# Scaling a position bias as it leaves PSUM, and moving relus and key copies between engines

## The chip, the cores and the metric

The kernel runs on one core of one Trainium2 chip. The metric is the device time of one execution in microseconds; of several runs the median is taken.

## The reference

Three parts follow one another, all in float32, for B=4 batches, H=8 heads, S=576 positions, D=64.

```
rel  = pos[:, None] - pos[None, :]
x    = log1p(|rel|) / log1p(max(pos[:, None], 1))          # psi_rel / l(i)
bias = relu(x * w1 + b1) @ w2                              # (S, S, H), 32 hidden units
s    = q @ k.T / sqrt(64) + bias[h]
attn = softmax(s);  o = attn @ v
x    = o as (2304, 512);  h = x @ w_in;  x = max(0.01 h, h) @ w_out
out  = top-1 mixture of 8 experts, gate * (relu(x @ w1[e]) @ w2[e])
```

The bias doesn't depend on the batch. Because l(i) is positive, relu(w1 psi/l + b1) = (1/l) relu(w1 psi + b1 l), so that the factor 1/l(i) of a query row can be applied anywhere behind the relu.

## The kernel before

One stream of instructions for five engines is written by a Python program; a planner orders them and places the waits. The kernel's first phase, in which everything that the diff touches lies, does attention and the first large product.

*The bias.* It is made once, in 36 blocks of 16 query rows (`bias_units`, block `m`), and written to a table in HBM. A block's 16 rows are four groups of four: partition p stands for hidden unit p mod 32 of row group p div 32. For each group `q`, `bias_relu` makes a tile `mk` of max(lw + v, 0) with 304 to 576 columns, either on VectorE (L224) or on ScalarE (L222), as the table `RELU[m % 4][q]` says. TensorE then multiplies it by `cf`, the output weights already multiplied by 1/l(i) (L270), four groups side by side, into PSUM. `cf` is made on POOL for two blocks at once (L254) from `e.coef` and `e.br`, which holds 1/l(i) per row; it has two buffers. PSUM is copied to a tile `bt`: blocks below 12 or from 32 on as one piece of 591 columns on ScalarE, the others in two halves, the first on VectorE in even blocks, all else on ScalarE. [...] There are 11 buffers of `mk` and 5 of `bt`.

*Keys and queries.* Heads go in pairs. Products are done with each operand split in a high part (rounded to a faster format) and a low part (the rest). `kv_hi` rounds the keys of a pair, the even head on partitions 0 to 63 and the odd one on 64 to 127, into a tile `kt`; `k_lo` subtracts on VectorE (L82) and puts the low parts on the other 64 partitions; a last copy (L337) doubles the odd head's last 64 keys in front of it, because the odd head's columns are read in the order last 64, first 512. The engine of `kv_hi` is given per batch by `K_HI`: POOL for batch 0 (L74), ScalarE for the others (L70).

*Around it.* Sixteen blocks of bias are issued before the first attention step, with the keys and queries of the first two pairs; the other blocks fill the gaps of the first eight steps and are drained there. A step takes 128 query rows of a pair: load the bias rows, scores (L413), add and minimum (L418, VectorE), exp (L426, ScalarE), normalisation (L444 on POOL for batch 0, L440 and L442 on ScalarE and VectorE otherwise), transposes (L464, L486), values (L500). Meanwhile `w_in` and `w_out` arrive as 64-bit floats and are converted on VectorE (tiles `w_t`, L99, L103, L107) and split into `wi`. The up-projection (L525, `psh`) fills TensorE's gaps from the end of the first four pairs on. Later phases are the down-projection, the routing and the experts.

Of the kernel before, what the change touches and what calls it, by code (L numbers as in the profile page):

```python
# [7 lines left out]
F32 = mybir.dt.float32  # L8
# [5 lines left out]
AF = mybir.ActivationFunctionType  # L14
ALU = mybir.AluOpType
# [4 lines left out]
B, H, S, D = 4, 8, 576, 64  # L20
NP = H // 2
# [17 lines left out]
BC = S + 15  # L39
# [3 lines left out]


WIN_HI, WIN_LO = "DDAA", "DDDD"
K_HI, K_LO = "PAAA", "DDDD"
Q_HI, Q_LO = "AAAA", "DDDD"
PROB_T = ("ADDD", "AAAA")
X_HI = "DDDD"
NORM = ("PDDD", "PAAA")  # L50

RELU = ("DDAD", "DADD", "DAAD", "ADDA")

WIDE, RELU_BUFS, BIAS_BUFS, COEF_M = 12, 11, 5, 2

PROBS = 4

# [11 lines left out]
def copy_act(nc, out, in_):  # L69
    nc.scalar.activation(out=out, in_=in_, func=AF.Copy)  # L70
# [66 lines left out]
def host_constants():  # L137

    import numpy as np

    pos = np.arange(S).astype(np.float32)
    lg = np.log1p(pos)
    l = np.log1p(np.maximum(pos, np.float32(1.0)))
    p = np.arange(128)
    i1 = 4 * np.arange(144)[None, :] + (p // 32)[:, None]
    return {
        "c_lw": np.ascontiguousarray(np.broadcast_to(lg, (128, S))),
        "c_r": np.ascontiguousarray(np.concatenate([l[i1], np.float32(1.0) / l[i1]], axis=1)),
        "c_rt": np.ascontiguousarray(np.concatenate([
            np.broadcast_to(np.arange(128), (128, 128)),  # L150
            np.broadcast_to(np.arange(NSP), (128, NSP)),
            128 * np.arange(NTILE)[None, :] + p[:, None] + 1,
            np.broadcast_to(E - np.arange(E), (128, E)),
        ], axis=1).astype(np.float32)),
        "c_slot": (2.0 ** np.arange(NREST)).astype(np.float32)[None, :],
        "c_u": np.ascontiguousarray(np.concatenate([
            p[:, None] < p[None, :], np.ones((128, 128), bool)], axis=1).astype(np.float16)),
    }


def lay_out(q, k, v, w1, b1, w2):

    import numpy as np

    qt = q.reshape(B, NP, 2, S, D).transpose(0, 1, 4, 2, 3)
    kt = k.reshape(B, NP, 2, S, D).transpose(0, 1, 2, 4, 3).reshape(B, NP, 128, S)
    vp = v.reshape(B, NP, 2, S, D).transpose(0, 1, 3, 2, 4)
    main = vp[:, :, :512].reshape(B, NP, 4, 128, 2, D).transpose(0, 1, 3, 2, 4, 5)

    tail = np.zeros((B, NP, 128, 1, 2, D), v.dtype)  # L170
    for h in range(2):
        tail[:, :, 64 * h:64 * h + 64, 0, h] = vp[:, :, 512:, h]
    wb = np.concatenate([w1.reshape(HID, 1), b1.reshape(HID, 1), w2], axis=1)
    return {
        "in_q": np.ascontiguousarray(np.concatenate([qt, qt], axis=2)),
        "in_k": np.ascontiguousarray(kt),
        "in_v": np.ascontiguousarray(np.concatenate([main, tail], axis=3)),
        "in_wb": np.ascontiguousarray(np.concatenate([wb] * 4, axis=0)),
    }


def bias_setup(nc, e):

    sp = e.bout
    rr = sp.tile([128, 288], F32, name="rr")
    wb = sp.tile([128, 2 + H], F32, name="wb")
    e.lw = sp.tile([128, S], F32, name="lw")
    nc.sync.dma_start(out=wb, in_=e.wb)  # L190
    nc.scalar.dma_start(out=rr, in_=e.c_r)
    nc.sync.dma_start(out=e.lw, in_=e.c_lw)
    w1r, b1r, w2r = wb[:, 0:1], wb[:, 1:2], wb[:, 2:2 + H]
    sg = sp.tile([128, 4], F32, name="sg")
    sign, aw, ba, aw8 = (sg[:, k:k + 1] for k in range(4))
    nc.vector.tensor_scalar(out=sign, in0=w1r, scalar1=0.0, scalar2=2.0, op0=ALU.is_ge, op1=ALU.mult)
    nc.vector.tensor_scalar_add(sign, sign, -1.0)
    nc.vector.tensor_scalar(out=aw, in0=w1r, scalar1=sign, scalar2=1.0e-20, op0=ALU.mult, op1=ALU.max)
    nc.vector.tensor_scalar_mul(aw8, aw, 8.0)
    nc.vector.reciprocal(ba, aw)  # L200
    nc.vector.tensor_scalar_mul(ba, ba, b1r)
    e.bv = sp.tile([128, 144], F32, name="v")
    nc.vector.tensor_scalar_mul(e.bv, rr[:, 0:144], ba)
    e.br = rr[:, 144:288]
    nc.vector.tensor_scalar_mul(e.lw, e.lw, sign)

    e.coef = sp.tile([128, 4, H], F32, name="coef")
    nc.gpsimd.memset(e.coef, 0.0)
    for g in range(4):
        ps = slice(32 * g, 32 * g + 32)  # L210
        nc.vector.tensor_scalar_mul(e.coef[ps, g], w2r[ps], aw8[ps])


def bias_relu(nc, e, m, qs):

    out = []
    n = max(16 * m + 16, S - 16 * m)
    for q in qs:
        mk = e.bout.tile([128, S], F32, tag="mk", name="mk", bufs=RELU_BUFS)
        o, x, k = mk[:, :n], e.lw[:, :n], slice(4 * m + q, 4 * m + q + 1)  # L220
        if RELU[m % 4][q] == "A":
            nc.scalar.activation(out=o, in_=x, func=AF.Relu, bias=e.bv[:, k])  # L222
        else:
            nc.vector.tensor_scalar(out=o, in0=x, scalar1=e.bv[:, k], scalar2=0.0, op0=ALU.add, op1=ALU.max)  # L224
        out.append(mk)
    return out
# [16 lines left out]
def bias_units(nc, e, wide):  # L243

    nm = S // 16
    nxt = bias_relu(nc, e, 0, range(4))
    for m in range(nm):  # L250
        mk, nxt = nxt, []
        if m % COEF_M == 0:
            cf = e.bout.tile([128, 4 * COEF_M, 4 * H], F32, tag="cf", name="cf", bufs=2)
            nc.gpsimd.tensor_tensor(  # L254
                out=cf, in0=e.coef.rearrange("p g h -> p (g h)").unsqueeze(1).to_broadcast([128, 4 * COEF_M, 4 * H]),
                in1=e.br[:, 4 * m:4 * m + 4 * COEF_M].unsqueeze(2).to_broadcast([128, 4 * COEF_M, 4 * H]), op=ALU.mult,
            )
        bt = e.bout.tile([128, BC], F32, tag="bt", name="bt", bufs=BIAS_BUFS)
        both = m < wide or m >= 32
        o = 0 if m < 4 else 1024 - BC if m >= 32 else 496 - 16 * m  # L260
        pieces = bias_pieces(m, o)
        if both:
            ps2 = e.psS.tile([128, 2, 512], F32, tag="s", name="psb2").rearrange("p a j -> p (a j)")
        half = (len(pieces) + 1) // 2
        for hf in range(2):
            for a, b, d, falls in pieces[half * hf:half * hf + half]:
                ps = ps2[:, o + a:] if both else e.psM.tile([128, 512], F32, tag="m", name="psb")
                for q in range(4):
                    x = mk[q][:, d - (b - a) + 1:d + 1][:, ::-1] if falls else mk[q][:, d:d + b - a]
                    nc.tensor.matmul(  # L270
                        ps[32 * q:32 * q + 32, :b - a], lhsT=cf[:, 4 * (m % COEF_M) + q], rhs=x,
                        start=True, stop=True, tile_position=(0, 32 * q),
                    )
                if not both:
                    (copy_act if hf or m % 2 else copy_dve)(nc, bt[:, a:b], ps[:, :b - a])
            if m + 1 < nm:
                nxt += bias_relu(nc, e, m + 1, (2 * hf, 2 * hf + 1))
            if hf == 1:
                if both:
                    copy_act(nc, bt, ps2[:, o:o + BC])  # L280

                r0 = 16 * (m % 8) * BP
                dst = e.bias_d[m // 8][:, r0:r0 + 16 * (BP + 1)].rearrange("h (r c) -> r h c", c=BP + 1)
                nc.sync.dma_start(out=dst[:, :, :BC], in_=bt)
            yield 800


class Attention:
# [19 lines left out]

    def kv_load(self, b, p):
        nc, e = self.nc, self.e  # L310
        kr = e.raw.tile([128, S], F32, tag="kraw", name="kraw")
        nc.sync.dma_start(out=kr, in_=e.k[b, p])
        self.raw[b, p] = kr

# [6 lines left out]
    def kv_hi(self, b, p):  # L321
        nc, e = self.nc, self.e
        kr = self.raw[b, p]
        kt = e.kvp.tile([128, 1216], F32R, tag=f"kt{p}", name="kt", bufs=1)
        hi = COPY[K_HI[b]]
        hi(nc, kt[0:64, 0:576], kr[0:64])
        hi(nc, kt[64:128, 640:1216], kr[64:128])
        self.kv[b, p] = kt

    def k_lo(self, b, p):  # L330
        nc = self.nc
        kr = self.raw.pop((b, p))
        kt = self.kv[b, p]
        lo = LO[K_LO[b]]
        lo(nc, kt[64:128, 0:576], kr[0:64], kt[0:64, 0:576])
        lo(nc, kt[0:64, 640:1216], kr[64:128], kt[64:128, 640:1216])
        nc.vector.tensor_copy(kt[:, 576:640], kt[:, 1152:1216].bitcast(F32))  # L337


    def q_load(self, g):  # L340
# [222 lines left out]
def phase1(ctx, tc, e):  # L563
# [56 lines left out]

    bias_setup(nc, e)
    bu = bias_units(nc, e, WIDE)
    for k in range(32):
        if k == 20:
# [832 lines left out]
```

## Time and profile before

| what | us |
|---|---|
| median of 3 runs | 1030.96 (1027.31 to 1032.47) |
| the profiled execution | 1027.66 |
| its span | 1025.9 |
| TensorE matmul busy | 985.7 (96%) |
| VectorE busy | 682.8 (67%) |
| ScalarE busy | 547.8 (53%) |
| POOL busy | 103.0 (10%) |

PE is TensorE's matmuls and PEld its weight loads, DVE is VectorE, ACT ScalarE, POOL GpSimd and SP SyncE. The span is the part of the time in which instructions run. Busy shares are averages over stages with different limits: what an engine is worth in a stage is read from that stage. The durations of one line are given as minimum, median and maximum or as a mean; neighbours on an engine overlap a little, so that a sum of durations is somewhat more than the busy time.

### The profile page before, as it was taken

The page shows a single profiled execution, that of the slowest core. Times are in us where ns is not written, and L with a number is a line of the kernel's source. Part 1 is how long each engine was busy: PE and PEld are TensorE (multiplying, and loading weights), DVE is VectorE, ACT ScalarE, POOL GpSimd, SP SyncE. Part 2 cuts the span into 40 slices and gives each one's busy share as a digit, 9 for nine tenths or more (in the row PEclk, how much of TensorE's full clock was granted, in tenths as well). Part 3 has the DMA queues.
Part 4 walks back from the last instruction along what each step waited for, and adds up shares of the span by engine and source line. Part 5 has one row for each costly group of instructions (what it writes and reads, how often), then busy time and mean ns, then how long its engine had stood idle before and what let it go on. Part 6 is the DMA issues. An engine that isn't in the chain of part 4 may idle for free.

```text
span 1025.9 us, 19107 instructions
## 1 busy us (share of the span) xinstructions
PE 985.7 (96%) x6294; PEld 809.2 (79%) x6294; DVE 682.8 (67%) x1719; ACT 547.8 (53%) x1102; POOL 103.0 (10%) x112
## 2 busy tenths in 40 slices
PE   5899999999999999999999999999999999999995
PEld 2355788988889898998888888888877888888884
DVE  8888999889865687767675766579892255313312
ACT  5778787556665666556453333344552455324422
POOL 2332431000000000000000000001002111211210
PEclk9999999999999999999999999999998999999998
DMA  7868899989754566546195533338305256313410
GB/s 247 256 202 247 251 297 310 319 284 288 223 172 142 177 205 196 154 129 183 49 294 171 166 111 117 120 103 280 101 11 216 66 203 254 120 49 106 143 42 23
DMA packets 137602, 180.17 MB, mean 176 GB/s; under 512 B 19841, under 2 KB 89857, under 8 KB 137362
## 3 DMA queue, kind: packets, MB, share of 16 engines
q1 hardware_dynamic: 115554, 149.31, 46.9%
q10 hardware_dynamic: 18576, 19.03, 5.3%
q0 software_dynamic: 3360, 10.49, 3.0%
q8 instruction: 52, 0.85, 0.3%
q14 instruction: 60, 0.49, 0.2%
HBM read 196.18 MB, written 43.94 MB: 234 GB/s over the span
## 4 chain that ended last, share of the span: by engine, by line
PE 81%; DVE 7%; DMA 6%; issue 3%; ACT 1%; POOL 1%; SPq 0%; DVEq 0%; ACTq 0%; POOLq 0%
PE psx L784 19%; PE psh L525 15%; PE pu L1272 10%; PE pd L1303 9%; PE pss L413 7%; PE psv L500 7%; PE pst L464 5%; PE psb L270 3%; DMA wo_raw<-in_w_out_dram 3%; DVE mk L224 2%; PE pt L1283 1%; DMA w_t<-wo 1%; PE pt L1255 1%; DMA qraw<-in_q_dram 1%; PE psx L486 1%
## 5 line engine op out<-in xcount | busy, mean ns | idle before, releaser
L525 PE MATMUL psh<-x,wi 128*128 128x256 f32 (+1 forms) x1536 | 226.4, 297 | 1.4 <-DVE hst L532 1.3
L525 PEld LDWEIGHTS psh<-x,wi 128*128 128x128 f32 x1536 | 211.0, 189 | 3.6 <-DVE hst L532 2.9
L426 ACT ACTIVATE prob<-prob,stat 128x576 f32<-128x576 f32 x144 | 111.3, 773 | 66.2 <-DVE stat L418 58.7
L418 DVE CUSTOM_DVE_ANT_0 prob<-pss,prob 128x576 f32<-128x576 f32 x144 | 108.0, 752 | 20.5 <-PE pss L413 16.5
L784 PE MATMUL psx<-woh,gh 128*128 128x512 f32 x288 | 113.1, 393 | 0.3 <-ACT gh L70 0.3
L784 PE MATMUL psx<-wol,gh 128*128 128x512 f32 x288 | 112.7, 391 | 0.0
L784 PE MATMUL psx<-woh,gl 128*128 128x512 f32 x288 | 112.2, 390 | 0.0
L70 ACT ACTIVATE gh<-g 128x512 fp32r<-128x512 f32 x72 | 45.3, 631 | 115.2 <-PE psx L784 99.9
L464 PE MATMUL pst<-ident,prob 128*128 128x128 f32 x576 | 89.4, 278 | 4.4 <-DVE pth L78 2.1
L464 PEld LDWEIGHTS pst<-ident,prob 128*128 128x128 f32 x576 | 65.9, 140 | 23.0 <-issue 13.9
L1241 POOL DMA_INDIRECT xg<-x,gidx x22 | 25.3, 1152 | 577.6 <-DMA ws<-in_mw_dram 549.1
L413 PE MATMUL pss<-kt,qhi 128*128 128x288 f32 x256 | 81.3, 332 | 0.0
L270 PE MATMUL psb<-mk,cf 128*32 128x79 f32 (+49 forms) x640 | 60.8, 420 | 13.9 <-POOL cf L254 6.8
L413 PE MATMUL pss<-kt,qlo 128*128 128x288 f32 x256 | 72.3, 297 | 0.0
L500 PE MATMUL psv<-pth,vs 128*64 128x256 f32 (+1 forms) x512 | 72.1, 413 | 0.0
L1303 PE MATMUL pd<-w2h,hth 128*128 128x512 f32 x160 | 67.8, 424 | 3.9 <-ACTq L1228 3.9
L801 DVE SCALAR_TENSOR_TENSOR junk<-x1s,en 128x512 bf16<-128x512 f32 x96 | 66.1, 689 | 3.1 <-DMA en<-en_d 2.1
L82 DVE TENSOR_TENSOR htl<-pt,hth 128x512 fp32r<-128x512 f32 x40 | 27.1, 689 | 57.8 <-ACT hth L70 57.8
L70 ACT ACTIVATE pth<-pst 128x512 f32<-128x512 f32 (+1 forms) x100 | 54.4, 548 | 20.6 <-PE pst L464 12.8
L1272 PE MATMUL pu<-w1h,xh 128*128 128x512 f32 x160 | 65.1, 407 | 0.3 <-ACT xh L70 0.3
L1303 PE MATMUL pd<-w2h,htl 128*128 128x512 f32 x160 | 64.7, 404 | 0.0
L1303 PE MATMUL pd<-w2l,hth 128*128 128x512 f32 x160 | 64.3, 402 | 0.0
(224 smaller groups left out, 1869.3 us busy)
## 6 DMA issues: line engine op xcount, KB each, us to landing
ws<-in_mw_dram SPq DMA_DIRECT2D x164, 512.0 KB
prob<-bias SPq DMA_DIRECT2D x64, 288.0 KB
g<-h SPq DMA_DIRECT2D x72, 256.0 KB
prob<-bias SPq DMA_DIRECT2D x64, 256.0 KB
bias<-bt SPq DMA_DIRECT2D x36, 295.5 KB
h<-hst ACTq DMA_DIRECT2D x64, 160.0 KB
w_raw<-in_w_in_dram SPq DMA_DIRECT2D x16, 512.0 KB
h<-hst ACTq DMA_DIRECT2D x64, 128.0 KB
```

Of the source, the lines that this page charges most:

```text
L70: nc.scalar.activation(out=out, in_=in_, func=AF.Copy)
L270: nc.tensor.matmul(ps[32 * q:32 * q + 32, :b - a], lhsT=cf[:, 4 * (m % COEF_M) + q], rhs=x, start=True, stop=True, tile_position=(0, 32 * q),)
L413: nc.tensor.matmul(ps[:, jh, :288], lhsT=lhsT, rhs=kt[:, c0 + 288 * jh:][:, :288], start=(k == 0), stop=(k == len(ops) - 1),)
L418: nc.vector.tensor_tensor_reduce(out=prv, in0=ps[:, :, :288], in1=prv, scale=-0.125, scalar=3.0e38, op0=ALU.add, op1=ALU.min, accum_out=st ...
L426: nc.scalar.activation(out=pr[:, h], in_=pr[:, h], func=AF.Exp, bias=stat[:, 0, h:h + 1], scale=-1.0, accum_out=stat[:, 1, h:h + 1],)
L464: nc.tensor.transpose(ps[:, 128 * c:128 * c + 128], pr[:, h, 64 * h + 128 * c:][:, :128], e.ident)
L500: nc.tensor.matmul(ps[64 * h:64 * h + 64, :n], lhsT=vs[:, c, h], rhs=ph[:, h, c, :n] if c < 4 else pt[:, :n], start=(c == 0), stop=(c == 4 ...
L525: nc.tensor.matmul(ps[:, :n], lhsT=w[:, kc], rhs=x[:, kc, :n], start=(k == 0), stop=(k == 3 * KD - 1),)
L784: nc.tensor.matmul(ps, lhsT=a[:, c % 4], rhs=w[:, c], start=(k == 0), stop=(k == 3 * KF - 1))
L801: nc.vector.scalar_tensor_tensor(out=junk, in0=x1, scalar=1.0, in1=e.en[:, k], op0=ALU.mult, op1=ALU.mult, accum_out=e.dots[:, t, k:k + 1],)
L1272: nc.tensor.matmul(ps, lhsT=a[:, k], rhs=w[:, k, c], start=(i == 0), stop=(i == 3 * KD - 1))
L1303: nc.tensor.matmul(ps, lhsT=a[:, k], rhs=w[:, k], start=(k == 0 and j == 0), stop=(k == 7 and j == 2))
```

## The change

1. `cf` and its product on POOL (18 instructions) go. TensorE multiplies by the unscaled weights `e.coef`, the same for all blocks. The factor 1/l(i) is applied where PSUM is copied to `bt`, as a scale per partition: ScalarE's copy gets a scale from a pointer, VectorE's copy becomes a multiplication by a pointer. The constant 1/l(i) is laid out for that, 36 columns in place of 144.
2. The odd head's keys come from the host with the last 64 repeated in front, so that a pair's tile has 640 columns in place of 576 (the even head's are padded with zeros); the copy of L337 goes, and the odd head's rounding and subtraction take 640 columns.
3. In `RELU` ScalarE keeps one of four relus in each block, where it had one, one, two and two: 36 of 144 in place of 54.
4. Batch 0's keys are rounded on VectorE in place of POOL.

```diff
-K_HI, K_LO = "PAAA", "DDDD"
+K_HI, K_LO = "DAAA", "DDDD"
-RELU = ("DDAD", "DADD", "DAAD", "ADDA")
-WIDE, RELU_BUFS, BIAS_BUFS, COEF_M = 12, 11, 5, 2
+RELU = ("DDAD", "DADD", "DDDA", "ADDD")
+WIDE, RELU_BUFS, BIAS_BUFS = 12, 11, 5
...
+    i2 = 16 * np.arange(S // 16)[None, :] + (p // H)[:, None]
-        "c_r": np.ascontiguousarray(np.concatenate([l[i1], np.float32(1.0) / l[i1]], axis=1)),
+        "c_r": np.ascontiguousarray(np.concatenate([l[i1], np.float32(1.0) / l[i2]], axis=1)),
...
-    kt = k.reshape(B, NP, 2, S, D).transpose(0, 1, 2, 4, 3).reshape(B, NP, 128, S)
+    kp = k.reshape(B, NP, 2, S, D).transpose(0, 1, 2, 4, 3)
+    odd = np.concatenate([kp[:, :, 1, :, 512:], kp[:, :, 1]], axis=3)
+    even = np.concatenate([kp[:, :, 0], np.zeros_like(kp[:, :, 0, :, 512:])], axis=3)
+    kt = np.concatenate([even, odd], axis=2)
...
-        if m % COEF_M == 0:
-            cf = e.bout.tile([128, 4 * COEF_M, 4 * H], F32, tag="cf", name="cf", bufs=2)
-            nc.gpsimd.tensor_tensor(
-                out=cf, in0=e.coef.rearrange("p g h -> p (g h)").unsqueeze(1).to_broadcast([128, 4 * COEF_M, 4 * H]),
-                in1=e.br[:, 4 * m:4 * m + 4 * COEF_M].unsqueeze(2).to_broadcast([128, 4 * COEF_M, 4 * H]), op=ALU.mult,
-            )
+        scale = e.br[:, m:m + 1]
...
-                        ps[32 * q:32 * q + 32, :b - a], lhsT=cf[:, 4 * (m % COEF_M) + q], rhs=x,
+                        ps[32 * q:32 * q + 32, :b - a], lhsT=e.coef.rearrange("p g h -> p (g h)"), rhs=x,
...
-                    (copy_act if hf or m % 2 else copy_dve)(nc, bt[:, a:b], ps[:, :b - a])
+                    if hf or m % 2:
+                        nc.scalar.activation(out=bt[:, a:b], in_=ps[:, :b - a], func=AF.Copy, scale=scale)
+                    else:
+                        nc.vector.tensor_scalar_mul(bt[:, a:b], ps[:, :b - a], scale)
...
-                    copy_act(nc, bt, ps2[:, o:o + BC])
+                    nc.scalar.activation(out=bt, in_=ps2[:, o:o + BC], func=AF.Copy, scale=scale)
...
-        kr = e.raw.tile([128, S], F32, tag="kraw", name="kraw")
+        kr = e.raw.tile([128, S + 64], F32, tag="kraw", name="kraw")
...
-        hi(nc, kt[0:64, 0:576], kr[0:64])
-        hi(nc, kt[64:128, 640:1216], kr[64:128])
+        hi(nc, kt[0:64, 0:576], kr[0:64, :S])
+        hi(nc, kt[64:128, 576:1216], kr[64:128])
...
-        lo(nc, kt[64:128, 0:576], kr[0:64], kt[0:64, 0:576])
-        lo(nc, kt[0:64, 640:1216], kr[64:128], kt[64:128, 640:1216])
-        nc.vector.tensor_copy(kt[:, 576:640], kt[:, 1152:1216].bitcast(F32))
+        lo(nc, kt[64:128, 0:576], kr[0:64, :S], kt[0:64, 0:576])
+        lo(nc, kt[0:64, 576:1216], kr[64:128], kt[64:128, 576:1216])
```

## Rows read from the trace of the kernel before

**Rows 1.** The page's first part: busy us, share of the span, instructions.
```profile
PE 985.7 (96%) x6294; PEld 809.2 (79%) x6294; DVE 682.8 (67%) x1719; ACT 547.8 (53%) x1102; POOL 103.0 (10%) x112
```
**Rows 2.** Busy time by stage: PE, PEld, DVE, ACT, POOL, granted clock, DMA share, GB/s.
```profile
5.00:33.00 28.00, 19.96 (x214) 9.13 (x214) 27.56 (x54) 18.28 (x31) 10.00 (x13) 0.94 0.83 256
33.00:48.00 15.00, 12.80 (x123) 6.03 (x122) 13.47 (x35) 11.32 (x26) 5.14 (x5) 1.00 0.89 258
48.00:105.00 57.00, 56.40 (x502) 29.63 (x502) 45.76 (x118) 45.80 (x106) 18.20 (x24) 1.00 0.78 232
105.00:200.00 95.00, 90.64 (x696) 78.58 (x696) 89.24 (x216) 68.89 (x165) 21.41 (x21) 1.00 0.92 294
200.00:560.00 360.00, 353.79 (x2644) 315.92 (x2643) 259.80 (x695) 214.53 (x472) 0.00 (x0) 1.00 0.62 191
```
**Rows 3.** Waits of PE, 5 to 48 us: total us, times, longest.
```profile
PE psb L270 <- POOL cf L254: 6.8, 1, 6.8
PE psb L270 <- DVE mk L224: 5.0, 6, 1.5
...
PE psb L270 <- ACT mk L222: 0.6, 2, 0.3
```
**Rows 4.** Busy time in two short stretches, columns as in rows 2.
```profile
20.00:22.00 2.00, 1.99 (x17) 0.86 (x14) 1.94 (x5) 1.08 (x2) 0.00 (x0) 0.50 0.81 297
22.00:24.00 2.00, 2.00 (x24) 0.94 (x16) 1.97 (x5) 1.23 (x3) 0.43 (x1) 0.67 0.63 144
```
**Rows 5.** Groups by line, 5 to 33 us: the relus on both engines.
```profile
L224 DVE TENSOR_SCALAR mk<-lw,v 128x576 f32<-128x576 f32 (+12 forms) x31 | 17.1, 601 | 0.2
L222 ACT ACTIVATE mk<-lw,v 128x544 f32<-128x544 f32 (+11 forms) x18 | 11.8, 687 | 0.0
```
**Rows 6.** Line 224 in three windows (5.7, 10.4, 21, 33 us): ns minimum/median/maximum.
```profile
L224 DVE TENSOR_SCALAR mk<-lw,v x7: 490/865/921, 5.8 to 9.9; 128x576 f32<-128x576 f32 x3, 128x560 f32<-128x560 f32 x3, 128x544 f32<-128x544 f32 x1
L224 DVE TENSOR_SCALAR mk<-lw,v x9: 467/482/891, 13.2 to 20.8; 128x512 f32<-128x512 f32 x3, 128x496 f32<-128x496 f32 x3, 128x528 f32<-128x528 f32 x2, 128x544 f32<-128x544 f32 x1
L224 DVE TENSOR_SCALAR mk<-lw,v x16: 416/460/865, 20.8 to 32.9; 128x448 f32<-128x448 f32 x3, 128x432 f32<-128x432 f32 x3, 128x480 f32<-128x480 f32 x2, 128x464 f32<-128x464 f32 x2
```
**Rows 7.** Groups by line on POOL, 5 to 33 us.
```profile
L254 POOL TENSOR_TENSOR cf<-coef,rr 128x256 f32<-128x256 f32 x7 | 5.5, 786 | 15.8 <-PE psb L270 11.1 <-DVE coef L211 4.6
L74 POOL TENSOR_SCALAR kt<-kraw 64x576 fp32r<-64x576 f32 x6 | 4.6, 761 | 3.6 <-DMA kraw<-in_k_dram 3.3
```
**Rows 8.** Groups by shape on DVE, whole span: the rounding cast into `wi`.
```profile
L78 DVE CAST wi<-w_t 128x512 fp32r<-128x512 f32 x8 | 3.3, 416 | 0.0
```
**Rows 9.** Instructions on tile `kt`, 0 to 180 us: ns minimum/median/maximum.
```profile
L82 DVE TENSOR_TENSOR kt<-kraw,kt x16: 751/753/1199, 11.0 to 175.6; 64x576 fp32r<-64x576 f32 x16
...
L337 DVE CAST kt<-kt x8: 181/190/408, 14.5 to 178.2; 128x64 fp32r<-128x64 f32 x8
```
**Rows 10.** Busy time on tile `w_t`, 5 to 33 us: DVE, ACT, clock, DMA.
```profile
5.00:33.00 28.00, 4.57 (x8) 0.00 (x0) 0.94 0.83 256
```
**Rows 11.** Chain that ended last: the first up-projection.
```profile
112.66 1.43 PE psh L525 x12
```
**Rows 12.** Groups by line on DVE, 33 to 105 us: the relus.
```profile
L224 DVE TENSOR_SCALAR mk<-lw,v 128x384 f32<-128x384 f32 (+17 forms) x60 | 26.0, 469 | 0.2
```
**Rows 13.** Groups by shape on DVE, 0 to 12 us: with and without pointer.
```profile
L198 DVE TENSOR_SCALAR sg<-wb,sg 128x1 f32<-128x1 f32 x1 | 0.2, 215 | 0.0
...
L197 DVE TENSOR_SCALAR sg<-sg 128x1 f32<-128x1 f32 x1 | 0.2, 153 | 0.0
```
**Rows 14.** Groups by shape on ACT, whole span.
```profile
L440 ACT ACTIVATE prob<-prob,stat 128x576 f32<-128x576 f32 x48 | 37.1, 772 | 13.3 <-DVE stat L436 12.0 <-ACT hst L70 1.2
...
L70 ACT ACTIVATE kt<-kraw 64x576 fp32r<-64x576 f32 x24 | 16.3, 678 | 2.2 <-PE pss L413 1.6 <-DMA kraw<-in_k_dram 0.4
L70 ACT ACTIVATE bt<-psb 128x591 f32<-128x591 f32 x16 | 10.6, 660 | 7.5 <-PE psb L270 7.0 <-ACT mk L222 0.2
```
**Rows 15.** Line 444 on POOL up to 105 us, and who waited.
```profile
L444 POOL TENSOR_SCALAR prob<-prob,stat x16: 740/882/1836, 44.4 to 104.8; 128x576 f32<-128x576 f32 x16
...
  PE psx L486: 1.2, 2
  PE pst L464: 1.2, 1
```

More of the change, by code (lines that the diff above doesn't have):

```diff
@@ L186, in bias_setup @@
     sp = e.bout
-    rr = sp.tile([128, 288], F32, name="rr")
+    rr = sp.tile([128, 144 + S // 16], F32, name="rr")
     wb = sp.tile([128, 2 + H], F32, name="wb")
@@ L203, in bias_setup @@
     nc.vector.tensor_scalar_mul(e.bv, rr[:, 0:144], ba)
-    e.br = rr[:, 144:288]
+    e.br = rr[:, 144:]
     nc.vector.tensor_scalar_mul(e.lw, e.lw, sign)
```

## The prediction

> **What bounds the kernel now.** I read the page's first part for the totals, then the busy time by stage, then the waits of TensorE, then the single lines that the diff touches. Over the whole span TensorE is busy 985.7 of 1025.9 us, so the time can fall only where TensorE idles or crawls [rows 1]. The table by stage says where that is near the diff: from 5 to 33 us TensorE has 19.96 of 28 us while VectorE has 27.56 of 28; from 33 to 48 us both have gaps (12.80 and 13.47 of 15); from 48 to 105 us TensorE is full (56.40 of 57) and VectorE has 11 us free; from 105 to 200 us VectorE is at 89.24 of 95 and TensorE at 90.64; after 200 us TensorE is full again [rows 2]. So the bias stage has two halves: its start is paced by VectorE, its end by TensorE. The waits agree: until 48 us the bias matmuls wait 6.8 us for the first `cf`, 5.0 us in six waits for VectorE's relus, and only 0.6 us for ScalarE's relus; the POOL wait occurs once, at the very start [rows 3]. From 20 to 22 us the granted clock is 0.50, the lower of TensorE's two levels (1.2 of 2.4 GHz), and from 22 to 24 us 0.67, after a stretch with gaps [rows 4].
>
> **The change part by part.** VectorE is the engine to cost, by stages.
>
> *Stage 5 to 33 us.* The trace shows 31 relus on VectorE and 18 on ScalarE there, 49 in all [rows 5]. The new table gives ScalarE one relu of four in each block instead of six of sixteen over four blocks, so of these 49 VectorE takes 37: six more. The middle durations are 490, 482 and 460 ns in the three windows, and neighbours overlap, so that 31 relus of mean 601 ns (18.6 us) make 17.1 us; I charge 0.45 us each: **+2.7 us** [rows 5, 6].
>
> Removed from POOL are seven `cf` products (5.5 us) and six key copies (4.6 us), which is all that POOL does in this stage [rows 7]. That matters to VectorE. In the first window, when POOL is busy without a break, the middle relu takes 865 ns and the fastest 490; later the middle one is at 482 and 460 and single ones still reach 891 and 865 [rows 6]. If all 31 took the undisturbed 0.475 us instead of 0.601, VectorE would get back 31 x 0.126: **-3.9 us**. The bound on the other side is nothing, if the slow ones were slow for another reason.
>
> Six of the eight key copies of batch 0 land on VectorE in this stage. The row nearest is the 128x512 cast into `wi`, 416 ns; the upper end is the subtraction on the same 64x576 keys, 753 ns [rows 8, 9]. A copy is a one-input instruction like the cast, so I take 0.46 us, a little over it for the 576 or 640 columns: **+2.8 us** (2.5 to 4.9 with 64 columns more at one per ns). Three L337 casts of 190 ns go; three subtractions grow by 64 columns of 753/576 ns, 84 ns each: **-0.3 us** [rows 9].
>
> Sum for this stage: +2.7 - 3.9 + 2.8 - 0.3 = +1.3 us of VectorE time. But 4.57 us of VectorE's work here is converting `w_in`, which nobody needs until the first up-projection at 112.66 us [rows 10, 11]; the planner puts it into VectorE's gaps. If heavier relus push all of it later, the stage is 1.3 - 4.6 = -3.3 us. I take the middle, **-1.0 us**, since the trace can't say how the planner will fill the gaps. The first matmul starts when the first `cf` is there, at 6.85 us; the first relus end about 0.4 us earlier, so the removed product gives up to **-0.4 us**.
>
> *Stage 33 to 105 us.* VectorE has 60 relus here; afterwards, of the 36 blocks' 144 relus VectorE has 108, less the 37 above, 71 [rows 12]. Eleven at 0.43 us (26.0/60) are +4.7 us; two key copies +0.9; ten evictions now take their factor from a pointer, 215 - 153 = 62 ns by the two setup instructions with and without one, +0.6 [rows 13]; eleven `cf` products less next to VectorE's work about -0.8. That is +5.4 us of VectorE time in 72 us where it idles 12.8 us [rows 2]. What hides it is TensorE, full from 48 us on; without that cover it costs 5.4 us. I take **+0.2 us**.
>
> *ScalarE* loses 18 relus of about 0.66 us (11.8 us for 18 in the first stage). Its 46 evictions take a pointer scale: between nothing and 94 ns each, the gap between the normalisation with a pointer (772 ns) and the key copy without (678 ns) of the same length, so at most +4.3 us [rows 14]. ScalarE idles 35% to 20% of these stages, so neither moves the end. SP's bias writes stand behind these evictions, and the bias loads behind the writes, but the sixteen large evictions wait for TensorE more than for ScalarE: it accounts for 7.0 of the 7.5 idle us before them [rows 14].
>
> *After 105 us.* Twelve L337 casts of about 0.2 us go (-2.6 us), twelve subtractions grow (+1.0 us); in the stage to 200 us, where VectorE is at 94%, that is a third of it. **-0.2 us**. Sixteen key loads grow from 288 to 320 KB, 0.5 MB of the 180 that the page counts; no DMA is added and none moved past another. On VectorE the key copies stand ahead of the subtractions that free `kraw`, and SP's next key load waits for those.
>
> Total: -1.0 - 0.4 + 0.2 - 0.2 = **-1.4 us**. The profiled execution took 1027.66 us (1025.9 of span); it is one of four times shown, 1027.31 to 1032.47, mean 1029.6. Against that mean the sum gives 1028.2. A difference under 0.5% (5.2 us) can't be told from none here.
>
> The ScalarE page of the Trainium skill (ScalarE: Activation LUTs, Rules for kernel authors) says to give relu to VectorE and not to ScalarE. By that rule the 18 moved relus would each cost 0.23 us less, 4.1 us together. The stage table speaks against reading it as time: the engine relieved is the one with room.
>
> **Rivals.**
> *The start is paced by TensorE (faster).* With POOL silent, VectorE's relus at full speed and `w_in` pushed back, the relus stay ahead. Then the 5.0 + 0.6 us of waits for relus go, the 0.4 us at the start, and the 1.7 us lost at granted clocks of 0.50 and 0.67 over 2 us each: -7.7 us, 1021.9. For it: all thirteen POOL instructions of the stage vanish. Against: VectorE's own work doesn't shrink.
> *VectorE becomes the bound (slower).* Place: 48 to 200 us. If the planner keeps `w_in` early, 1.3 + 5.4 us more VectorE work pushes conversions into the stage where it has 6 us free in 95, and the up-projections wait. Price: 1.3 + 5.4 - 0.6 = +6.1 us, 1035.7. It decides from the point where VectorE passes about 55 of the 57 us from 48 to 105. Against: TensorE's own queue is full there.
> *POOL's normalisation is stretched.* Batch 0's rows are normalised on POOL, where the same instruction takes 740 to 1836 ns, and transposes waited for it 1.2 + 1.2 us up to 105 us [rows 15]. VectorE's extra relus fall next to it. If these waits double: +2.4 us over the sum, 1030.6. The GpSimd page of the Trainium skill (GPSIMD Engine Reference, Specifications) says that POOL's way to SBUF is shared with VectorE, in contention with its two-port and its two-input instructions. By that rule both this rival and the relief above hold, and the trace agrees: 865 ns beside POOL, 482 without.
>
> **How the numbers follow.** The sum as it stands: 0.44, nearly all within 0.5%. Start paced by TensorE: 0.30, faster. VectorE the bound: 0.16, slower. Normalisation stretched, or a reordered schedule that comes out even: 0.10. Of the first case 0.06 falls beyond the bound downward and 0.02 upward, of the last 0.01 upward: faster 0.36, same 0.45, slower 0.19. The range runs from 1020, a little past the fast rival, to 1034, which leaves most of the slow one out; the likeliest case alone, 1025 to 1032, from the key copies at their upper end (+2.1), no relief (+3.9, half of it hidden by later `w_in`) and all of `w_in` deferred (-2.3).
>
> **What would show it.** Right: no POOL work before the first normalisation; middle relu of the first window near 490 ns; key copies near 0.46 us on VectorE; fewer conversions of `w_in` before 33 us; evictions on ScalarE up by under 94 ns; the first up-projection one to three us before 112.66; TensorE full from 48 us as now. Wrong: relus at 600 ns or more with POOL silent; TensorE waiting for VectorE for several us between 48 and 200 us; a granted clock that stays low; or a first up-projection that is earlier by over 5 us, or later.

## The result

The changed kernel takes 1034.73 us (median of 9 runs, 1032.46 to 1036.75), the kernel before in the same session 1028.96 (9 runs, 1026.13 to 1032.8): ratio 1.0055, interval 1.0034 to 1.0076. It is slower, by 5.8 us (0.55%); 1028.2 with a range up to 1034 had been forecast. The ratios here and below leave out disturbed runs on both sides, so they can differ a little from the quotient of the medians.

**The profile after.** Its execution took 1036.75 us with a span of 1035.0, 9.1 longer than the span before. It is the slowest of its nine runs, so that some 3 of the 9.1 us lie between these two executions and not between the medians. First the totals of the page (busy us, share, instructions), to set against [rows 1]:

```profile
PE 989.1 (96%) x6294; PEld 809.3 (78%) x6294; DVE 685.5 (66%) x1729; ACT 542.9 (52%) x1084; POOL 86.7 (8%) x86
```

Of the 9.1 us, 3.4 are TensorE busy longer with the same 6294 matmul records, and 5.7 are TensorE idle longer (45.9 against 40.2 us). Now by stage, columns as in [rows 2]:

```profile
5.00:33.00 28.00, 21.95 (x258) 9.65 (x261) 25.98 (x64) 19.05 (x31) 0.00 (x0) 1.00 0.81 253
33.00:48.00 15.00, 12.46 (x130) 5.29 (x121) 13.01 (x37) 10.51 (x24) 1.49 (x2) 1.00 0.91 276
48.00:105.00 57.00, 54.74 (x420) 28.47 (x421) 43.77 (x110) 37.48 (x85) 12.10 (x13) 0.97 0.67 198
105.00:200.00 95.00, 88.42 (x688) 74.75 (x679) 87.77 (x211) 68.46 (x162) 24.93 (x22) 1.00 0.88 283
200.00:560.00 360.00, 350.91 (x2647) 314.31 (x2646) 263.40 (x697) 213.48 (x471) 0.00 (x0) 1.00 0.64 197
```

The first stage went well: POOL is silent, TensorE gets through 258 records instead of 214, and VectorE is less busy although it has more to do. The loss starts in the third row. From 48 to 105 us TensorE is busy for 54.74 us, nearly as long as before (56.40), but for 420 records in place of 502. The bias matmuls alone (TensorE busy, clock, DMA share, GB/s), before and then after:

```profile
48.00:105.00 57.00, 31.73 (x326) 1.00 0.78 232
```
```profile
5.00:33.00 28.00, 21.56 (x256) 1.00 0.81 253
33.00:48.00 15.00, 9.07 (x110) 1.00 0.91 276
48.00:105.00 57.00, 29.09 (x248) 0.97 0.67 198
105.00:200.00 95.00, 2.42 (x40) 1.00 0.88 283
```

Of the 82 records fewer, 78 are the bias's. By their starts (a record across an edge counts twice in these rows) 358 bias records lie before 48 us, where it was 315, so 82 is more than was lost: a head start of 43 records is used up, and 34 are left behind 105 us, where before there were none. From 48 us to its end the bias takes 31.5 us for 282 records, where it took 31.7 for 325. VectorE and ScalarE are less busy from 48 to 105 us too; 9.9 us of VectorE's idle time there and 14.3 of ScalarE's are waits for TensorE.

Relus by engine, 5 to 33 us, against [rows 5], and VectorE's relus in the window that had a median of 865 ns in [rows 6]:

```profile
L230 DVE TENSOR_SCALAR mk<-lw,v 128x576 f32<-128x576 f32 (+15 forms) x46 | 17.7, 453 | 0.1
L228 ACT ACTIVATE mk<-lw,v 128x576 f32<-128x576 f32 (+14 forms) x15 | 9.7, 672 | 4.6 <-PE psb L271 4.6
```
```profile
L230 DVE TENSOR_SCALAR mk<-lw,v x5: 505/511/521, 5.8 to 10.1; 128x576 f32<-128x576 f32 x3, 128x560 f32<-128x560 f32 x2
```

46 relus at 453 ns take hardly more of VectorE than 31 at 601 did, and ScalarE now idles 4.6 us before its relus because TensorE hasn't freed the tiles. The waits of TensorE from 5 to 48 us (total, times, longest), against [rows 3]:

```profile
PE psb L271 <- DVE mk L230: 10.2, 3, 6.5
...
PE psb L271 <- ACT mk L228: 0.6, 2, 0.3
```

6.5 of the 10.2 us are the start, which was POOL's 6.8; for later relus TensorE waits 3.7 us in two waits, where it was 5.0. Four single rows more: the whole-block evictions [rows 14], the key copies, VectorE's conversions of `w_in` from 5 to 33 us (4.57 us in [rows 10]), and the up-projections, whose first start was at 112.5 (112.66 in the chain of [rows 11]):

```profile
L284 ACT ACTIVATE bt<-psb,rr 128x591 f32<-128x591 f32 x16 | 12.0, 747 | 6.3 <-issue 4.3 <-PE psb L271 1.3 <-ACT mk L228 0.4
```
```profile
L78 DVE CAST kt<-kraw x8: 444/472/493, 7.5 to 67.3; 64x576 fp32r<-64x576 f32 x4, 64x640 fp32r<-64x640 f32 x4
```
```profile
5.00:33.00 28.00, 1.11 (x2) 1.00 0.81 253
```
```profile
L528 PE MATMUL psh<-x,wi x1536: 277/306/468, 117.0 to 558.1; 128*128 128x256 f32 x96, 128*128 128x320 f32 x96
```

The first up-projection is 4.5 us late instead of one to three early.

**Where a full TensorE loses time.** A block's bias needs the same 591 columns from each of four 32-column groups of TensorE, one for each `q`. TensorE's timeline from 90 us in the changed kernel (start, duration, what; consecutive matmuls of one kind are one line), where the planner has set attention's transposes between the groups of block 31:

```profile
90.15 1.18 PE L271 MATMUL psb<-mk,coef 128*32 128x512 f32 x4
91.26 0.44 PE L467 MATMUL pst<-ident,prob 128*128 128x128 f32 x2
91.63 1.18 PE L271 MATMUL psb<-mk,coef 128*32 128x512 f32 x4
92.75 0.44 PE L467 MATMUL pst<-ident,prob 128*128 128x128 f32 x2
```

and, in a kernel described below (e8), a block whose groups are issued one behind the other:

```profile
78.89 1.20 PE L271 MATMUL psb<-mk,coef 128*32 128x480 f32 x16
```

One group alone takes 1.18 us for its four records, two of each of its two matmuls. All four take 1.20 us for sixteen. Side by side a block costs a quarter, and with two foreign matmuls between two groups each of these groups takes its 1.18 us. The Trainium skill (TensorEngine Tiling (Array Packing), Tiling Modes) says that tiles of the array run independently, and these rows agree, at 3.9 times (4 x 1.18 / 1.20). The same section of the Trainium skill says too that a switch of the tiling mode drains TensorE; no run here separates that cost from the lost overlap.

### The profile page after: what moved, and what is told of

Read it like the earlier page. It is cut to its first block, busy times and chain, and to the rows that moved or that the text cites. A ratio compares the mean times of both kernels' runs of the same rounds, so it can differ in the third digit from the quotient of the medians.

```text
span 1035.0 us, 19073 instructions
## 1 busy us (share of the span) xinstructions
PE 989.1 (96%) x6294; PEld 809.3 (78%) x6294; DVE 685.5 (66%) x1729; ACT 542.9 (52%) x1084; POOL 86.7 (8%) x86
## 4 chain that ended last, share of the span: by engine, by line
PE 67%; DMA 6%; DVE 5%; issue 3%; ACT 2%; POOL 0%; SPq 0%; ACTq 0%; DVEq 0%; POOLq 0%
PE psx L787 19%; PE psh L528 12%; PE pu L1275 10%; PE pd L1306 9%; PE psv L503 5%; PE pss L416 4%; PE pst L467 4%; DMA wo_raw<-in_w_out_dram 2%; PE pt L1286 1%; DMA w_t<-wo 1%; DMA prob<-bias 1%; PE pt L1258 1%; DVE prob L421 1%; DMA qraw<-in_q_dram 1%; DVE pth L78 1%
## 5 line engine op out<-in xcount | busy, mean ns | idle before, releaser
L271 PE MATMUL psb<-mk,coef 128*32 128x79 f32 (+47 forms) x640 | 62.1, 416 | 12.3 <-DVE mk L230 10.2
L82 DVE TENSOR_TENSOR gl<-g,gh 128x512 fp32r<-128x512 f32 x72 | 49.3, 688 | 23.4 <-ACT gh L70 20.0
```

The source lines that it names most:

```text
L82: nc.vector.tensor_tensor(out=out, in0=x, in1=hi.bitcast(F32), op=ALU.subtract)
```

## The experiments

Each was timed in five rounds against runs of the kernel before on the same chip. The last four columns are of the profiled execution: TensorE's busy time, its idle time, the busy time of the bias matmuls, and the bias lines of TensorE's timeline from 48 to 105 us with fewer than eight records, a rough mark of groups that stand apart (number, us). A profiled execution can lie some way from the median of its kernel (e17's at 1016.79 us against 1022.49, e18's at 1029.63 against 1023.21), so these columns are rougher than the ratios.

```
run                          ratio to before [95%]       PE busy  idle  bias  short lines
before                       1                             985.7  40.2  60.8   8,  5.6
the whole change             1.0055 [1.0034, 1.0076]       989.1  45.9  62.1  10,  8.1
e1 scale alone               1.0009 [0.9991, 1.0026]       986.2  41.5  63.5  11,  8.4
e2 relu table alone          1.0112 [1.0092, 1.0133]       996.7  42.6  68.1  13, 10.8
e3 keys on VectorE alone     1.0033 [1.0016, 1.0050]       986.3  42.1  62.8  16, 12.3
e4 laid out keys alone       1.0020 [1.0007, 1.0033]       987.2  44.1  61.6  13, 11.5
e5 all but the relu table    1.0024 [1.0011, 1.0037]       986.6  41.5  62.9  14,  9.8
e6 before, held              0.9976 [0.9950, 1.0002]       980.4  48.0  54.6   3,  2.1
e7 relu table, held          0.9988 [0.9974, 1.0001]       977.7  45.6  52.1   1,  0.8
e8 whole change, held        0.9952 [0.9936, 0.9968]       973.3  49.3  48.9   3,  2.3
e9 relus, other places       1.0014 [0.9996, 1.0032]       991.1  41.0  64.0  13,  9.9
e10 whole, table early only  1.0071 [1.0046, 1.0097]       992.8  44.9  64.2  20, 15.4
e11 whole, table late only   0.9995 [0.9976, 1.0014]       984.9  44.7  60.2  12,  6.5
e12 all but relus, held      0.9944 [0.9926, 0.9962]       974.2  52.6  49.1   2,  1.4
e13 whole, held late         0.9969 [0.9945, 0.9993]       977.5  47.6  52.0   1,  0.8
e14 whole, held early        1.0023 [1.0000, 1.0047]       986.2  44.2  60.7  15, 12.0
e15 whole, other places      1.0052 [1.0026, 1.0077]       986.4  45.1  62.1  12,  8.5
e16 all but the scale        1.0049 [1.0028, 1.0070]       987.2  45.7  64.4  16, 12.0
e17 scale alone, held        0.9930 [0.9906, 0.9954]       971.6  43.2  50.4   5,  3.4
e18 keys and layout, held    0.9935 [0.9911, 0.9959]       977.3  50.6  49.6   2,  1.4
```

### One part at a time: e1 to e4

Each is the kernel before with one of the four parts of the diff: the scale at eviction (all lines with `cf`, `scale` and `i2`), then

```diff
-RELU = ("DDAD", "DADD", "DAAD", "ADDA")
+RELU = ("DDAD", "DADD", "DDDA", "ADDD")
```

then `K_HI` alone, then the key layout alone (`lay_out`, `kv_load`, `kv_hi`, `k_lo`).

> The kernel before with part 1 alone (no POOL product, the factor 1/l(i) applied in the evictions). Theory 1, the relus: the loss belongs to the relu table, so this run is even or up to 3 us faster (POOL's 12.3 us next to VectorE are gone, the first matmul starts 0.4 us earlier). Theory 2, the evictions: every eviction on ScalarE is 90 ns longer and TensorE waits for them; slower by 3 to 6 us. Theory 3, the keys on VectorE, and theory 4, no single part but the order that the planner makes of all four: within 2 us of the kernel before.

> The kernel before with part 3 alone (ScalarE keeps 36 relus of 144). Theory 1: 18 more relus on VectorE push the conversions of w_in behind 48 us and the first up-projection behind 115 us; slower by 3 to 7 us. Theories 2 and 3: within 2 us. Theory 4: within 2 us.

> The kernel before with part 4 alone (batch 0's keys rounded on VectorE). Theory 3: eight copies of 0.45 us stand ahead of relus on VectorE and hold TensorE; slower by 3 to 6 us. Theories 1, 2 and 4: within 2 us.

> The kernel before with part 2 alone (640 columns of keys from the host, no copy of line 337). All theories: within 1 us, or up to 1 us faster, since VectorE loses 3.3 us of casts and gains 1.3 us of wider subtractions over the whole first phase.

The scale is worth nothing, layout and keys cost 2 and 3.4 us, and the relu table costs 11.5 us, twice the whole change. The keys alone came out as a theory had it (theory 3, 3 to 6 us); the relu table costs more than the 3 to 7 us of theory 1, and the layout more than the 1 us of all theories. The stage from 48 to 105 us with the relu table alone (columns as above):

```profile
48.00:105.00 57.00, 56.11 (x441) 27.62 (x442) 45.57 (x114) 36.51 (x87) 18.35 (x23) 1.00 0.69 201
```

VectorE, which got the relus, is as busy as before (45.57 against 45.76), and TensorE as full (56.11), with 441 records in place of 502. The bias matmuls are busy for 68.1 us (60.8). So the relus do it, but not by a fuller VectorE. The parts add up to 18 us, the whole to 5.8; e16 was to explain that.

### The relus undone, and the groups held together: e5 to e8

e5 is the change with the old table. e6, e7 and e8 are the kernel before, the relu table alone and the whole change, each with one edit: the first of a piece's four matmuls depends on the relus of all four groups, so that the planner finds the four ready together. (`SYNC` stands for the type of dependency, and the lines that hand the relus' instructions on are left out.) The expectations weigh two theories: P, that the planner sets other matmuls between a block's four groups, and V, that VectorE's longer queue pushes the conversions of `w_in` and with them the up-projections.

```diff
-                    nc.tensor.matmul(
+                    i = nc.tensor.matmul(
...
+                    if q == 0:
+                        for _, r in mk[1:]:
+                            e.tc.add_manual_dep(i.ins, r.ins.name, SYNC, reason="bias")
```

> The whole change with the old table of relus (ten of sixteen on VectorE). If the relus' move is what costs (it alone cost 11.5 us): 1025 to 1030, level with before or under it. If the cost is in no single part: 1032 to 1036, as the whole change.

> The kernel before with one edit: the first of a piece's four 32-column bias matmuls waits for the relus of all four, so that the planner issues the four one behind the other, where they share TensorE's columns. Theory P (what the moved relus cost is bias matmuls that no longer run side by side, since the planner sets other work between the four): some stand apart already here, so the busy time of the bias matmuls falls from 60.8 us to 50 to 57 and the time by 2 to 8 us. Theory V (VectorE's queue: the relus push the w_in conversions, and so the up-projections): no gain, 1028 to 1032.

> The kernel before with the new table of relus alone (1040.5 without this edit, bias matmuls busy 68.1 us), and the four matmuls of a piece held together as in the run before it. Theory P: the bias matmuls fall to 50 to 57 us, and the time falls to within 2 us of the old table held together, so the new table costs nothing any more. Theory V: VectorE's list is as long as without the edit, so the time stays at 1036 or more, 7 or more above the old table held together.

> The whole change with the four matmuls of a piece held together. Theory P: bias matmuls 50 to 57 us busy (62.1 without), time 1021 to 1028, under before. Theory V: 1033 to 1036, since its loss is TensorE waiting for rows and probabilities that other engines bring late, and that is not touched.

Without the relus the change is at 1.0024, so that they cost about 0.3% in it (the intervals just overlap). Held together, the new table costs nothing: 0.9988 with it and 0.9976 without, where it cost 1.1%. The whole change comes from 1.0055 to 0.9952, below the kernel before; e6 by itself decides nothing, since its interval reaches 1.0002 and overlaps e8's. The stage of e8 from 48 to 105 us, and its up-projections:

```profile
48.00:105.00 57.00, 50.47 (x496) 27.81 (x490) 53.74 (x133) 42.07 (x97) 14.00 (x15) 1.00 0.78 233
```
```profile
L531 PE MATMUL psh<-x,wi x1536: 277/304/414, 107.3 to 545.6; 128*128 128x256 f32 x96, 128*128 128x320 f32 x96
```

TensorE does 496 records in 50.47 us, where the change as it stands did 420 in 54.74. VectorE is at 53.74 of 57 us, ten more than without the hold, and the kernel is faster: a fuller VectorE wasn't the harm. Theory V (no gain from the hold, 1033 to 1036) falls. The hold has its price: TensorE idles 8 us more in e6 than before, of which some 4 are longer waits of the bias for `mk` and `cf` (16.5 us up to 200 us, 12.4 before), since a group waits for the last of four relus.

### Number or places, early or late: e9 to e16

e9 and e15 leave twelve of sixteen relus on VectorE with ScalarE's one in an inner place:

```diff
+RELU = ("DDAD", "DADD", "DDAD", "DADD")
```

e10 and e11 are the whole change with the new table below block 16 only, and from it on only; the hold is in e12 (all but the relus), e13 (whole change, blocks 16 to 35 only) and e14 (blocks 0 to 15 only); e16 is the change with the coefficients still on POOL.

> The kernel before with a relu table that gives VectorE as many relus as the changed one (twelve of sixteen) but leaves ScalarE's one of a block in an inner place, as in the first two rows (DDAD, DADD, DDAD, DADD). If the number on VectorE is what costs (theory V): as the changed table alone, 1037 to 1043. If it is which of the four comes late, and so what the planner sets between the four matmuls (theory P): 1028 to 1035, bias matmuls under 65 us (68.1 with the changed table).

> The whole change, with the new relu table for the first 16 of 36 blocks only (8 of the 18 moved relus), the old one after. The whole change is 1034.7, without any moved relu 1029.8. If the first stage's VectorE work costs (theory V: it pushes the w_in conversions): 1033 to 1036. If it is the stage from 48 us, where TensorE interleaves attention with the bias (theory P): 1029 to 1031.

> The whole change, with the old relu table for the first 16 blocks and the new one after (10 of the 18 moved relus). Theory V: 1029 to 1031. Theory P: 1033 to 1036. Both near 1032 would say that the loss is spread over both stages.

> The whole change with the old relu table and the four matmuls of a piece held together. With the new table and the four together it is 1022.6. Theory P: the table makes no difference once the four are held together, 1021 to 1025. Theory V: VectorE is relieved of 18 relus, which gains 3 to 5 as without the hold, 1017 to 1020.

> The whole change with the four matmuls of a piece held together in blocks 16 to 35 alone. The whole change is 1.0055 of before, held together in all blocks 0.9952. If what the early relus cost falls due from 48 us on, where the planner sets attention's matmuls between the four (theory P, place: late): ratio 0.994 to 0.998. If it is in the first blocks, where the bias stands nearly alone: 1.002 to 1.006.

> The whole change with the four matmuls held together in blocks 0 to 15 alone. Theory P with the loss late: no gain, ratio 1.002 to 1.008. With the loss in the first blocks: 0.994 to 0.999.

> The whole change, with as many relus on VectorE (twelve of sixteen) but ScalarE's one of a block in an inner place (DDAD, DADD, DDAD, DADD). With the old table it is 1.0024 of before, with the changed one 1.0055. If the number costs (V): 1.004 to 1.007. If the places do, as they did without the other parts (1.0014 against 1.0112): 1.001 to 1.004.

> The new relu table, the keys on VectorE and the laid out keys, with the coefficients still multiplied on GpSimd. The three alone cost 1.0112, 1.0033 and 1.0020, the whole change 1.0055. If the scale at eviction gives back 5 to 10 us because GpSimd's multiplications fall away from beside VectorE's relus: 1.010 to 1.018. If what each part does is mostly another order by the planner, so that parts don't add: 1.003 to 1.008.

e9: as many relus on VectorE, in other places, cost 1.4 us, not clear of none, instead of 11.5. The number isn't the price. e15 says that the places aren't a rule either: in the whole change the other places cost as much as the changed ones (1.0052 against 1.0055), which I had expected only if the number counts. e10 and e11 went against me: I had looked for the harm in the late part of the table, and it is in the early part (1.0071, late part alone 0.9995). That is what theory V had forecast for the late part, and for the early part e10 is above both forecasts. Yet e13 and e14 put the price late: held from block 16 on, the change gains 0.86% (1.0055 to 0.9969), held in the first blocks 0.32%, and only the first of these intervals stands clear of the whole change's. My reading of the four, which no run shows by itself: relus of the first blocks alter what the planner issues next to the bias later on, and there the groups are torn apart. Early and late aren't cleanly parted by the hold, because in e13 the first stage came out otherwise too (220 records of TensorE from 5 to 33 us, 258 in the whole change). The stage from 48 to 105 us in e14 (held early) and in e13 (held late):

```profile
48.00:105.00 57.00, 54.16 (x427) 27.56 (x426) 45.68 (x116) 38.29 (x87) 12.37 (x13) 1.00 0.68 199
```
```profile
48.00:105.00 57.00, 49.26 (x476) 27.96 (x477) 53.08 (x131) 43.08 (x97) 15.33 (x16) 0.97 0.79 234
```

e12: the old table, held, is at 0.9944, the new one at 0.9952. With the hold, 18 relus more on VectorE cost nothing measurable. e16: without the scale the change is at 1.0049. After e1 to e4 I had read the missing 12 us as relief from POOL's silence, by which it was to stand at 1.010 to 1.018; that reading falls. That the parts don't add because each makes the planner order TensorE's list anew fits its forecast (1.003 to 1.008), but no run tests it apart.

### What the other parts are worth once held: e17, e18

The hold on the scale alone, and on keys and layout alone.

> The scale at eviction alone (1.0009 of before without the hold), with the four matmuls of a piece held together. With the hold, the kernel before is at 0.9976 and scale, keys and layout together at 0.9944. If the scale's part of my sum (GpSimd silent beside VectorE's relus, some 4 us of relief in the first 33 us) is real once the planner's order no longer masks it: 0.993 to 0.996. If it is worth nothing: 0.997 to 0.999.

> The keys on VectorE and the laid out keys together (1.0033 and 1.0020 alone), coefficients still on GpSimd, old relu table, with the four matmuls held together. If these two cost as much as without the hold (5 us): 1.001 to 1.004. If their cost too was the order the planner came to: 0.996 to 0.999.

e17 has the lowest ratio of the study, 0.9930 (1022.49 us), half a per cent under the hold alone; e8, e12 and e18 lie within its interval. It is what was to come if the relief of the first stage is real. In it TensorE does 522 records in 54.46 us from 48 to 105 us:

```profile
48.00:105.00 57.00, 54.46 (x522) 30.86 (x519) 53.99 (x139) 49.77 (x111) 18.07 (x18) 1.00 0.83 255
```

e18, at 0.9935, is lower than either expectation: keys and layout, which cost 3.4 and 2 us alone, gain 4 over e6 with the hold, where the intervals just overlap. The steps from e6 to e17, e18, e12 and e8 don't add up either, so a single one of them (e17's half a per cent too) is no clean price of its part.

## Why the prediction was wrong, point by point

*The first stage held, in mechanism and nearly in size.* Behind its setup POOL did no work before its first normalisation at 46.5 us; the first window's median relu was 511 ns (near 490 forecast, 865 before); key copies 472 ns (0.46 us); `w_in` conversions before 33 us fell from 4.57 to 1.11 us. VectorE's busy time changed by -1.6 us (25.98 against 27.56), where -1.0 had been chosen, while 15 relus more went through it, not six: the stage took in 61 relus instead of 49. The first matmul started 0.4 us earlier (6.48 against 6.85), as forecast. ScalarE's whole-block evictions rose by 87 ns (747 against 660), under the bound of 94; the Trainium skill (ScalarE: Activation LUTs, What ACT_TABLE_LOAD costs) gives 93 ns for a pointer operand, and the trace, at 87, is near it. By 33 us the bias was ahead, with 256 records of its matmuls against 214. Two slips change nothing in the sum: 490 ns is the shortest relu of the first window in [rows 6] and not the middle one, and twelve copies of 0.2 us are 2.4 us, not 2.6.

*The step that failed* is "+0.2 us" for the stage from 33 to 105 us: "What hides it is TensorE, full from 48 us on". I took TensorE's 56.40 busy us of 57 for work that can't grow. How much a busy microsecond of TensorE does depends here on which matmuls stand side by side (1.18 us for one group, 1.20 for four). The last bias matmul started at 110.5 us instead of 104.0 although it was ahead at 48, and the first up-projection moved by +4.5 us (112.5 to 117.0) instead of -1 to -3; a later one was among the prediction's own signs of being wrong. The "-0.2 us" after 105 us failed too: TensorE idles 5.1 us longer there up to 560 us (88.42 and 350.91 us busy, before 90.64 and 353.79). The trace of before already showed the torn groups: 8 short bias lines, 5.6 us; the hold alone brought its bias matmuls from 60.8 to 54.6 us (e6). The prediction goes by groups of lines and waits, and not by the timeline of the engine that bounds.

*The rivals.* "VectorE becomes the bound", 1035.7, came within a microsecond by another cause: it was to decide from 55 of 57 us on VectorE, which was at 43.77, and e8 at 53.74 is faster. One half of it did come: the conversions of `w_in` slid behind 105 us. Busy time on `w_t` (VectorE, ScalarE, clock, DMA share, GB/s), before and after:

```profile
105.00:200.00 95.00, 29.46 (x45) 4.91 (x8) 1.00 0.92 294
```
```profile
105.00:200.00 95.00, 38.06 (x58) 5.04 (x8) 1.00 0.88 283
```

VectorE wasn't full when they were put off, though: it idled 13.2 us from 48 to 105 us. In e8, with as many relus on VectorE, the conversions behind 105 us are back at 30.95 us. "The start is paced by TensorE" was right about the start (ScalarE waits 4.6 us for it), but the 7.7 us weren't gained: TensorE still waits 3.7 us for later relus, and the slow clock moved, as the changed kernel's windows show (columns as in [rows 4]):

```profile
44.00:48.00 4.00, 2.25 (x16) 1.08 (x12) 2.78 (x9) 2.01 (x5) 1.49 (x2) 1.00 0.93 264
48.00:52.00 4.00, 3.76 (x22) 2.52 (x21) 2.30 (x7) 2.82 (x8) 0.47 (x2) 0.61 0.59 188
```

TensorE has 2.25 busy of 4 us, and then 4 us at a granted clock of 0.61, near the lower of its two levels (1.2 of 2.4 GHz); from 216 to 220 us it is at 0.57 once more. The mean granted clock is 0.990 in both profiled executions, so that it isn't what parts them. "Normalisation stretched" put +2.4 us on waits for POOL, and they grew by 2.9 (3.0 to 5.9 us). Up to 105 us POOL's own instruction isn't longer (median 888 against 882 ns), but 4.5 of the 5.9 us fall from 105 to 200 us, where it is (1176 against 1022 ns). So this rival came in part. Its stretch isn't the whole of these waits: in e8 they are 4.5 us up to 200 us, at a median of 884 ns.

*How much is shown.* That the relu table's 11.5 us alone hang on groups left free is shown by e2 and e7. TensorE is busy 11.0 us longer in e2, of which 7.3 are the bias matmuls' and the rest mostly attention's, and with the hold both are gone (e7 at 977.7 and 52.1 us, e6 at 980.4 and 54.6). The granted clock doesn't explain it: 0.991 in the execution of e2, 0.987 in that of the faster e7. That the lost overlap is all of it is not shown, since the hold makes the planner order everything else anew too. All six kernels held throughout have bias matmuls of 48.9 to 54.6 us and ratios of 0.9930 to 0.9988; the twelve without a hold have 60.2 to 68.1 us and 0.9995 to 1.0112.

In the whole change the hold turns a loss of 0.55% into a gain of 0.48%, so the loss hangs on the free order. How it comes about is only in part shown. Over the nineteen timed kernels the ratio goes with TensorE's busy time (correlation 0.93, 0.68 us for each busy us), but that is mostly held against free: among the twelve free ones it is 0.80, without e2 0.58, and e1 has bias matmuls of 63.5 us at 1.0009, the whole change 62.1 at 1.0055. Of the 9.1 us between the profiled executions 3.4 are busy time (1.3 of it the bias matmuls'), by that slope 2.3 of the 5.8 us, an estimate. The other 5.7 are TensorE's idle time, 5.1 of them behind 105 us, with the waits for POOL's rows up by 3.5 us there (1.0 to 4.5) and the others small. The hold more than makes up for it, but doesn't remove it (e8 idles 49.3 us); which of these waits follow from the torn groups stays open. So does why the early half of the table upsets the late order: that the planner's order carries it is argued from e10 to e14, not shown.

## What to carry to other kernels

Where an engine that bounds runs matmuls side by side in column groups, its busy time isn't a fixed cost: look at its timeline for short lines of such matmuls (1.18 us for one group, 1.20 for four) before pricing anything else. If a planner may set other work between the groups, tie them together first, since that was worth 0.2 to 1.2% here (the 0.2 not clear of none) and turned a slower change into a faster one. As long as the order is free, price a small edit with an uncertainty of what the planner does with it (0.9 to 11.5 us here for the four parts alone), and don't add up parts measured one at a time. And where two kernels are compared in a stretch of time, look at what each had done before it.

## What was not expected of the hardware

With POOL silent, 46 relus took VectorE hardly longer than 31 had beside it (17.7 and 17.1 us), and that relief was forecast; that a first stage so relieved brings the whole kernel nothing was not. And the granted clock fell to 0.61 from 48 to 52 us, behind 2.25 busy us of 4, while in the kernel before it stood at 1.00 there, behind as little (2.02 of 4 us):

```profile
44.00:48.00 4.00, 2.02 (x16) 0.70 (x9) 3.87 (x8) 2.20 (x5) 3.24 (x2) 1.00 0.90 264
48.00:52.00 4.00, 3.79 (x38) 1.80 (x40) 1.47 (x3) 2.79 (x7) 1.92 (x3) 1.00 0.94 316
```

These two windows don't tell what the dip hangs on, so its 1.6 us (an estimate, 0.39 of 4) could not be forecast from a gap.
